# Gated linear attention and a rational feed-forward block on one core: a new order of the first loads, and 80 unread products ahead of the first sum

## The chip, the core and the metric

The kernel runs on one core of a Trainium2 chip. The engines of the core are TensorE (PE in the profile, its weight loads PEld), VectorE (DVE), ScalarE (ACT), GpSimd (POOL) and SyncE (SP). SyncE, ScalarE and GpSimd also issue DMA transfers, each into a queue of its own. The metric is device time in microseconds (us), the median of several executions of one program.

## What is computed

For each of 4 batches and 8 heads of width 48, a state of 48 by 48 numbers runs over 768 steps: it is multiplied by a gate and gets the outer product of k and v added, and q reads it. The result, 3072 rows of 384, goes through two matrix products with a rational function between them.

```python
f = 1.0 / (1.0 + np.exp(-f_logit))
for t in range(S):
    state = f[:, :, t, :, None] * state + np.einsum('bhd,bhe->bhde', k[:, :, t], v[:, :, t])
    y[:, :, t] = np.einsum('bhd,bhde->bhe', q[:, :, t], state)
...
h = x @ w_in                                   # 3072x384 by 384x2048
P = a[0] + a[1] * h + a[2] * h2 + a[3] * h3
Q = 1.0 + np.abs(b[0]) * np.abs(h) + np.abs(b[1]) * h2
return (P / (Q + 1e-06)) @ w_out               # 3072x2048 by 2048x384
```

## The kernel before

The work is cut into 12 units of 256 steps of one batch (3 stretches of time by 4 batches). A unit is done in chunks, so that the recurrence becomes matrix products. Its steps, by the names that the order uses:

- `ld n f|k|q|v` loads an input of unit n. An input lies in the memory as 8 heads; the numbers behind it (`0 2`, `2 4`) pick half of the heads. f, k and q are issued by SyncE; v is issued by GpSimd and is turned into bf16 on its way.
- `ef`, `ls` (ScalarE, L289 and L294): exponential and logarithm of the gate. `cs` (TensorE, L304, L308, L312): the running sums of these logarithms by products with triangular matrices `Ui` and `Us`; L312 is a group of products with only 4 columns. `A` (ScalarE, L326): exponentials of the sums.
- `xa n x` (VectorE or GpSimd, L331): k (x = 1) or q (x = 0) times `A`, into the tile `qkp`. `T` transposes it on TensorE (L345), `Te` copies it back, `sc` forms scores (L368), `mk` masks them (VectorE, L376). `ic` and `si` form the new state (TensorE, L434 and L444), `st` scales it (VectorE, L459). `yb` and `yi` form the output rows (L389), `ye` writes them out as `x`.
- `h` (TensorE, L469) is the product with `w_in`; 16 blocks of 128 columns, so `h 0 8 12` is blocks 8 to 11 of unit 0. Steps on VectorE, ScalarE and accumulating DMAs make the rational function, `o` (L549) is the product with `w_out`, `so` the store.
- `wi a 8 16` loads one of four row groups of the second half of `w_in` (L215, GpSimd); the first product `h 0 8 12` needs all four. `ab_ b` and `ab_ a` load the coefficients (L226), `fa` works on b.
- `cu 0`, `cu 1` and `ci` build `Ui`, `Us` and the identity on GpSimd; `cz` and `cm` fill zeros and the mask on VectorE.

The order of all steps is written out by hand in one table, `ORDER`. Each engine runs its own instructions in the order of the table, and waits by semaphores. `!m0` behind a step sets a mark, `^m0` behind another makes its DMA wait until the marked step is done. `@3` is the PSUM slot (of four) that a step takes. The first five rows of the table of before are these; the whole first unit, and the beginning of the second, lie in them:

```python
cu 1; cz 1; ld 0 f 2 4; ld 0 v; ab_ b s; cz 3; cz 0; ld 0 f 0 2; ci; ld 0 q 2 4; ld 1 f; cu 0; ld 0 k 0 2
ef 0 2 4; ls 0 2 4; cm; ld 0 k 2 4; cz 2; fa; cs 0 2 4 @0; ef 0 0 2; ls 0 0 2; ld 0 q 0 2; cs 0 0 2 @1; ld 1 k
A 0 1 0 2; A 0 1 2 4; A 0 0 2 4; A 0 0 0 2; fr; ld 2 f; ef 1; xa 0 1 2 4; ls 1; xa 0 0 2 4; vm 0 v; cs 1 @2
xa 0 0 0 2; ld 1 q; xa 0 1 0 2 !m0; ld 1 v ^m0; ld 3 f; ic 0 @3; wi 2 8 16; A 1 1; wi 3 8 16; A 1 0
T 0 0 2 @0; st 0 0; ld 2 q; ab_ a s; wi 1 8 16; xa 1 1 2 4; T 0 2 4 @1; wi 0 8 16; Te 0 0 2 s; sc 0 0 @2
```

So the load of v of unit 1 waits until the last product `xa 0 1 0 2` of unit 0, and the four loads of `w_in` stand behind it in GpSimd's queue.

Of the kernel before, what the change touches and what calls it, by code (L numbers as in the profile page):

```python
# [8 lines left out]
F32 = mybir.dt.float32  # L9
# [7 lines left out]


ORDER = """
cu 1; cz 1; ld 0 f 2 4; ld 0 v; ab_ b s; cz 3; cz 0; ld 0 f 0 2; ci; ld 0 q 2 4; ld 1 f; cu 0; ld 0 k 0 2  # L20
ef 0 2 4; ls 0 2 4; cm; ld 0 k 2 4; cz 2; fa; cs 0 2 4 @0; ef 0 0 2; ls 0 0 2; ld 0 q 0 2; cs 0 0 2 @1; ld 1 k
A 0 1 0 2; A 0 1 2 4; A 0 0 2 4; A 0 0 0 2; fr; ld 2 f; ef 1; xa 0 1 2 4; ls 1; xa 0 0 2 4; vm 0 v; cs 1 @2
xa 0 0 0 2; ld 1 q; xa 0 1 0 2 !m0; ld 1 v ^m0; ld 3 f; ic 0 @3; wi 2 8 16; A 1 1; wi 3 8 16; A 1 0
T 0 0 2 @0; st 0 0; ld 2 q; ab_ a s; wi 1 8 16; xa 1 1 2 4; T 0 2 4 @1; wi 0 8 16; Te 0 0 2 s; sc 0 0 @2
xa 1 0 0 2; Te 0 2 4 s; xa 1 0 2 4; ef 2; si 0 1; sc 0 1 @0; xa 1 1 0 2; st 0 1; T 1 @1; mk 0 0; ld 2 k
mk 0 1; yb 0 0 2 @3; yi 0 1; Te 1; ef 3; yb 0 2 4; ic 1 @2; ls 2; st 1 0 !m1; sc 1 1 @0; ld 2 v ^m1; ye 0 s
cs 2 @1; mk 1 1 !m4; ls 3; sc 1 0 @3; wi 0 0 8; A 2 0; si 1 1; ld 5 f; cs 3 @0; wi 3 0 8; st 1 1; A 2 1
# [75 lines left out]
def _at(t, dims, off=0):  # L103

    return bass.AP(tensor=t.tensor, offset=t.offset + off, ap=[t.ap[0]] + [list(d) for d in dims])
# [3 lines left out]
def kernel(  # L109
# [12 lines left out]
    nc = tc.nc  # L122
    B, H, S, D = q.shape
    C = 128
    P = 128
# [23 lines left out]
    Us = consts.tile([P, P], BF16, name="Us")  # L149
# [37 lines left out]
    def unit(n):  # L187
        if n not in units:
            c, b = divmod(n, B)
            units[n] = dict(n=n, c=c, b=b, qk=qkp[n % 2], ls=lsp[n % 2], vm=vmp[n % 2])  # L190
        return units[n]
# [5 lines left out]
    def slot(i, shape, dtype, name):  # L197
        return slots[i].tile(shape, dtype, name=name, tag="s")
# [46 lines left out]
    def const_z(i):  # L245
        if i < 2:
            nc.vector.memset(lsp[i][:, :, :, D:E], 0.0)
            nc.vector.memset(qkp[i].rearrange("p x i h d -> p (x i h) d")[:, :, D:E], 0.0)
            nc.vector.memset(vmp[i][:, :, :, 16:32], 0.0)
        elif i == 2:  # L250
            nc.vector.memset(ind, 0.0)
            for j in range(UB):
                nc.vector.memset(ind[R * j:R * j + R, j, :], 1.0)
        else:
            nc.vector.memset(hsel, 0.0)
            for r in range(2):
                nc.vector.memset(hsel[E * r:E * r + E, :, :, 1 - r], 1.0e4)
# [199 lines left out]
    def st(n, j):  # L457
# [3 lines left out]
            s["sv"][:, j].rearrange("p (b w) (r d) -> p b (w r) d", b=2, r=2),  # L461
            _at(s["ae"], [[DM + 16 if n else DM // 2 + 8, 2], [1, 4], [0, D]], 4 * j))

    def h(n, m0, m1, sl):
        s = unit(n)
        t = s["hp", m0] = slot(sl, [P, 4, NT], F32, "hp")
        for m in range(m0, m1):
            for kk in range(KD):
                nc.tensor.matmul(t[:, m - m0, :].rearrange("f (j t) -> f j t", j=UB),  # L469
                                 w_in_sb[:, kk, m * P:(m + 1) * P], s["x"][:, :, kk, :],  # L470
                                 start=(kk == 0), stop=(kk == KD - 1))
# [98 lines left out]
    def behind(i, mark):  # L570
# [2 lines left out]
                          reason="begins behind it")  # L573

    steps = dict(ld=load, wi=load_w_in, wo=load_w_out, ab_=load_ab, cu=const_u, ci=const_i, cm=const_m,
                 cz=const_z, fa=coef_a, fb=coef_b, fr=coef_r, tab=tab, ef=ef, ls=ls, cs=cs, A=A, xa=xa, T=T, Te=Te,
                 sc=sc, mk=mk, vm=vm, yi=yi, yb=yb, ic=ic, si=si, ye=ye, st=st, h=h, hy=hy, sq=sq, sa=sa, ab=ab,
                 zv=zv, zd=zd, rq=rq, p1=p1, p2=p2, pm=pm, ta=ta, tv=tv, gm=gm, o=o, oe=oe, so=store)
    for step in ORDER.replace("\n", ";").split(";"):
# [41 lines left out]
```

## Time and profile before

| | |
|---|---|
| median of 3 runs | 210.68 us (208.77 to 211.42) |
| profiled execution | 210.19 us |
| its span, from the first to the last instruction | 208.5 us |
| instructions on TensorE | 2894 products, 2894 weight loads |
| DMA traffic | 43.15 MB, 207 GB/s on the mean |

The profile is of one execution. A row of its timeline gives the start, the busy time, the engine, the source line and the operation, then how many instructions were merged into the row; in square brackets stands how long the engine was idle ahead of it and what ended that wait. "issue" means that nothing which the profile records ended it. Times in such rows count from the start of the span; the profiled execution's own time is 1.69 us more than its span.

### The profile page before, as it was taken

The page shows a single profiled execution, that of the slowest core. Times are in us where ns is not written, and L with a number is a line of the kernel's source. Part 1 is how long each engine was busy: PE and PEld are TensorE (multiplying, and loading weights), DVE is VectorE, ACT ScalarE, POOL GpSimd, SP SyncE. Part 2 cuts the span into 40 slices and gives each one's busy share as a digit, 9 for nine tenths or more (in the row PEclk, how much of TensorE's full clock was granted, in tenths as well). Part 3 has the DMA queues.
Part 4 walks back from the last instruction along what each step waited for, and adds up shares of the span by engine and source line. Part 5 has one row for each costly group of instructions (what it writes and reads, how often), then busy time and mean ns, then how long its engine had stood idle before and what let it go on. Part 6 is the DMA issues. An engine that isn't in the chain of part 4 may idle for free.

```text
span 208.5 us, 6605 instructions
## 1 busy us (share of the span) xinstructions
PE 191.0 (92%) x2894; PEld 139.4 (67%) x2894; DVE 187.0 (90%) x235; ACT 186.1 (89%) x172; POOL 77.8 (37%) x99
## 2 busy tenths in 40 slices
PE   1297799989999999999999999999999999999991
PEld 1165487867767778766888677678766766776650
DVE  3378579999999999999999989999999999999970
ACT  4756389999999999999999999999999999999871
POOL 6060610516961535026151760641674433412000
PEclk9999699999999999999999999999999999999998
DMA  6999999799999499999999999899999999998955
GB/s 98 287 300 186 271 220 253 186 220 233 168 206 202 85 176 152 249 267 265 208 222 252 250 199 229 209 200 210 185 191 163 214 211 195 193 190 183 238 146 167
DMA packets 61820, 43.15 MB, mean 207 GB/s; under 512 B 51424, under 2 KB 56544, under 8 KB 61792
## 3 DMA queue, kind: packets, MB, share of 16 engines
q0 software_dynamic: 20528, 23.86, 69.3%
q1 hardware_dynamic: 41184, 18.78, 34.7%
q8 instruction: 22, 0.36, 0.6%
q10 hardware_dynamic: 80, 0.10, 0.2%
q14 instruction: 6, 0.05, 0.1%
HBM read 25.17 MB, written 4.72 MB: 143 GB/s over the span
## 4 chain that ended last, share of the span: by engine, by line
PE 75%; DVE 10%; DMA 6%; SPq 4%; issue 2%; ACT 1%; DVEq 0%
PE op L549 31%; PE hp L469 26%; PE y L389 6%; SPq L209 4%; PE cs L304 3%; DMA v<-in_v_dram 3%; PE tp L345 3%; PE sc L368 2%; DMA q<-in_q_dram 2%; DVE scm L376 2%; DVE g L528 2%; PE sv L434 2%; DVE state L459 1%; PE sv L444 1%; DVE qkp L331 1%
## 5 line engine op out<-in xcount | busy, mean ns | idle before, releaser
L549 PE MATMUL op<-w_out_sb,g 128*128 128x384 bf16 x384 | 68.6, 326 | 0.0
L469 PE MATMUL hp<-x,w_in_sb 128*128 128x256 bf16 x576 | 68.0, 273 | 0.3 <-DVE state L459 0.3
L469 PEld LDWEIGHTS <-w_in_sb 128*128 128x128 bf16 x576 | 55.4, 98 | 9.4 <-issue 0.7
L549 PEld LDWEIGHTS <-g 128*128 128x128 bf16 x384 | 35.8, 98 | 22.6 <-DVE g L540 0.4
L481 ACT CAST hy<-hp 128x1024 bf16<-128x1024 f32 x48 | 47.8, 1027 | 2.6 <-PE hp L469 2.3
L508 ACT ACTIVATE z<-z 128x4096 bf16<-128x4096 bf16 (+1 forms) x16 | 44.5, 2780 | 1.1 <-DVE z L499 1.1
L540 DVE TENSOR_TENSOR g<-g,z 128x2048 bf16<-128x2048 bf16 (+2 forms) x24 | 28.9, 1218 | 1.1 <-issue 0.6
L503 POOL DMA_DIRECT2D z<-h x20 | 20.6, 1077 | 24.7 <-ACT h L490 17.0
L528 DVE TENSOR_TENSOR g<-g,h 128x2048 bf16<-128x2048 bf16 (+1 forms) x21 | 28.8, 1373 | 0.1
L376 DVE TENSOR_TENSOR scm<-sc,mask 128x1024 bf16<-128x1024 f32 x24 | 28.8, 1216 | 0.0
L490 ACT ACTIVATE h<-hy 128x2048 bf16<-128x2048 bf16 (+1 forms) x13 | 26.8, 2073 | 0.0
L326 ACT ACTIVATE A<-cs 128x768 f32<-128x768 f32 (+3 forms) x26 | 19.0, 779 | 6.5 <-PE cs L312 6.5
L532 POOL DMA_DIRECT2D g<-hy x15 | 13.8, 943 | 28.3 <-DVE g L528 9.3
L304 PE MATMUL cs<-lsp,Ui 128*128 128x384 bf16 (+1 forms) x39 | 12.0, 371 | 10.1 <-ACT lsp L294 8.7
L518 DVE TENSOR_SCALAR g<-hy,a_sb 128x2048 bf16<-128x2048 bf16 (+1 forms) x23 | 18.9, 829 | 1.4 <-ACT hy L481 1.4
L331 POOL TENSOR_TENSOR qkp<-k,A 128x384 bf16<-128x384 f32 x11 | 11.0, 1025 | 23.6 <-DVE g L540 10.4
L523 DVE TENSOR_SCALAR hy<-hy,a_sb 128x2048 bf16<-128x2048 bf16 (+1 forms) x20 | 18.3, 915 | 0.4
L209 POOL DMA_DIRECT2D v<-in_v_dram x12 | 12.1, 1012 | 15.7 <-DVE qkp L331 8.3
L494 DVE TENSOR_SCALAR z<-hy 128x2048 uint16<-128x2048 uint16 (+1 forms) x21 | 15.8, 764 | 0.0
L459 DVE TENSOR_TENSOR state<-sv,A 128x384 bf16<-128x384 f32 x20 | 11.0, 552 | 4.5 <-PE sv L444 2.4
L389 PE MATMUL y<-scm,v 64*32 64x128 bf16 x384 | 14.0, 218 | 0.8 <-DVE scm L376 0.7
L331 POOL TENSOR_TENSOR qkp<-q,A 128x384 bf16<-128x384 f32 x10 | 10.0, 1010 | 11.5 <-ACT A L326 5.5
(70 smaller groups left out, 246.4 us busy)
## 6 DMA issues: line engine op xcount, KB each, us to landing
z<-h POOLq DMA_DIRECT2D x20, 512.0 KB, 7.5
g<-hy POOLq DMA_DIRECT2D x15, 512.0 KB, 7.8
f<-in_f_logit_dram SPq DMA_DIRECT2D x11, 384.0 KB, 5.8
k<-in_k_dram SPq DMA_DIRECT2D x11, 384.0 KB, 7.7
q<-in_q_dram SPq DMA_DIRECT2D x11, 384.0 KB, 7.8
v<-in_v_dram POOLq DMA_DIRECT2D x12, 192.0 KB, 7.7
out_dram<-f SPq DMA_DIRECT2D x12, 192.0 KB, 3.9
out_dram<-osb SPq DMA_DIRECT2D x10, 192.0 KB, 6.4
```

Of the source, the lines that this page charges most:

```text
L209: return eng.dma_start(out=s[what][:, hh].rearrange("p h i d -> p h (i d)"), in_=src[s["b"], hh, t0:t0 + NT, :].rearrange("h (p i) d -> p ...
L331: i = (nc.gpsimd if eng == "p" else nc.vector).tensor_mul(s["qk"][:, x, :, hh, 0:D], s["qk"[x]][:, hh].rearrange("p h i d -> p i h d"), s[ ...
L376: return nc.vector.tensor_mul(t, s["sc", g].rearrange("s r a i t -> s (r a) (i t)"), mb)
L389: nc.tensor.matmul(s["y"][32 * a:32 * a + 32, j, kk * C:kk * C + C].rearrange("e (i t) -> e i t", i=2), lhsT, rhs, start=(j, a) not in s[" ...
L469: nc.tensor.matmul(t[:, m - m0, :].rearrange("f (j t) -> f j t", j=UB), w_in_sb[:, kk, m * P:(m + 1) * P], s["x"][:, :, kk, :], start=(kk ...
L481: nc.scalar.copy(fl(big(s, "hy"), m0, m1), fl(s["hp", m0], 0, m1 - m0))
L490: return nc.scalar.activation(fl(big(s, "h2"), m0, m1), fl(big(s, "hy"), m0, m1), AF.Square)
L503: return nc.gpsimd.dma_start(out=fl(big(s, "z"), m0, m1), in_=fl(big(s, "h2"), m0, m1), accum_op=ALU.add)
L508: return nc.scalar.add_instruction(mybir.InstActivation(name=nc.get_next_instruction_name(), func=AF.Reciprocal, ins=[nc.scalar.lower_ap(f ...
L528: return nc.vector.tensor_mul(fl(big(s, "g"), m0, m1), fl(big(s, "g"), m0, m1), fl(big(s, "h2"), m0, m1))
L540: return nc.vector.tensor_mul(fl(big(s, "g"), m0, m1), fl(big(s, "g"), m0, m1), fl(big(s, "z"), m0, m1))
L549: nc.tensor.matmul(s["op", g][:, j, 0:DM], big(s, "g")[:, m, C * j:C * j + C], w_out_sb[:, m, :], start=(s["on", j] == 1), stop=(s["on", j ...
```

## The change

Three things, all in the first five rows of `ORDER`, and one new step:

- The loads of unit 0 stand in another order: both halves of f, then k and q of the second half, f of unit 1, then q and k of the first half. b is loaded by ScalarE and no longer by SyncE. v of unit 0 is issued behind the building of `Ui` and of the identity, and `Ui` is built ahead of the identity.
- The mark `m0`, behind which v of unit 1 is loaded, moves from the step `xa 0 1 0 2` to `st 0 0`.
- A step `dn 80 @3` stands ahead of `cs 0 2 4`: 80 products of `Us` with 4 of its own columns into PSUM slot 3. Nothing reads them.

```diff
-cu 1; cz 1; ld 0 f 2 4; ld 0 v; ab_ b s; cz 3; cz 0; ld 0 f 0 2; ci; ld 0 q 2 4; ld 1 f; cu 0; ld 0 k 0 2
+cu 1; cz 1; ld 0 f 2 4; ab_ b a; cu 0; cz 3; cz 0; ld 0 f 0 2; ci; ld 0 v; ld 0 k 2 4; ld 0 q 2 4; ld 1 f
...
-T 0 0 2 @0; st 0 0; ld 2 q; ab_ a s; wi 1 8 16; ...
+T 0 0 2 @0; st 0 0 !m0; ld 1 v ^m0; wi 2 8 16; wi 3 8 16; ld 2 q; ab_ a s; wi 1 8 16; ...
...
+    def dn(n, sl):
+        t = slot(sl, [P, 2, 512], F32, "dn")
+        for i in range(n):
+            nc.tensor.matmul(t[:, i % 2, 0:4], Us, Us[:, 0:4], start=True, stop=True)
...
-                 cz=const_z, fa=coef_a, fb=coef_b, fr=coef_r, tab=tab, ef=ef, ls=ls, cs=cs, A=A, xa=xa, T=T, Te=Te,
+                 cz=const_z, fa=coef_a, fb=coef_b, fr=coef_r, tab=tab, ef=ef, ls=ls, cs=cs, dn=dn, A=A, xa=xa, T=T, Te=Te,
```

On SyncE, at the start of the program, the rows move as follows. f_117, k_120 and q_123 are the tiles of unit 0, f_118 and k_121 those of unit 1; a row with `4x96` is half of the heads.

```order
-L209 DMA f_117<-in_f_logit_dram 128x4x96
-L226 DMA b_sb<-in_moe_b_dram 128x2
-L209 DMA f_117<-in_f_logit_dram 128x4x96
+L622 UNCONDITIONAL_BRANCH
+L209 DMA f_117<-in_f_logit_dram 128x4x96 x2
+L209 DMA k_120<-in_k_dram 128x4x96
 L209 DMA q_123<-in_q_dram 128x4x96
 L209 DMA f_118<-in_f_logit_dram 128x8x96
-L209 DMA k_120<-in_k_dram 128x4x96 x2
 L209 DMA q_123<-in_q_dram 128x4x96
+L209 DMA k_120<-in_k_dram 128x4x96
```

The load of b is gone from this queue, the second half of f stands directly behind the first, and the first half of k has moved behind the first half of q.

On GpSimd, at the start, v_126 is v of unit 0, v_127 that of unit 1.

```order
-L209 DMA v_126<-in_v_dram 128x8x96
-masks.py:197 MEMSET ident 128x128
-masks.py:199 AFFINE_SELECT ident<-ident 128x128
 masks.py:65 MEMSET Ui 128x128
 masks.py:66 AFFINE_SELECT Ui<-Ui 128x128
 L232 AFFINE_SELECT Ui<-Ui 128x128
+masks.py:197 MEMSET ident 128x128
+masks.py:199 AFFINE_SELECT ident<-ident 128x128
+L209 DMA v_126<-in_v_dram 128x8x96
 L209 DMA v_127<-in_v_dram 128x8x96
 L215 DMA w_in_sb<-in_moe_w_in_dram 32x3x1024 x4
```

Only the load of v_126 and the building of the identity have moved; v_127 and the four loads of `w_in` behind it stand where they stood, and what has changed for them is the step that v_127 waits for.

On TensorE the 160 new rows stand ahead of everything else; the last of them, with what follows, read:

```order
L468 LDWEIGHTS Us
L468 MATMUL dn<-Us 128x4
L304 LDWEIGHTS Ui
L304 MATMUL cs<-lsp_81,Ui 128x192
```

Behind them the order of TensorE is that of before, each row 160 places further on in its program.

More of the change, by code (lines that the diff above doesn't have):

```diff
@@ L19 @@
 ORDER = """
-cu 1; cz 1; ld 0 f 2 4; ld 0 v; ab_ b s; cz 3; cz 0; ld 0 f 0 2; ci; ld 0 q 2 4; ld 1 f; cu 0; ld 0 k 0 2
-ef 0 2 4; ls 0 2 4; cm; ld 0 k 2 4; cz 2; fa; cs 0 2 4 @0; ef 0 0 2; ls 0 0 2; ld 0 q 0 2; cs 0 0 2 @1; ld 1 k
+cu 1; cz 1; ld 0 f 2 4; ab_ b a; cu 0; cz 3; cz 0; ld 0 f 0 2; ci; ld 0 v; ld 0 k 2 4; ld 0 q 2 4; ld 1 f
+ef 0 2 4; ls 0 2 4; cm; ld 0 q 0 2; cz 2; fa; dn 80 @3; cs 0 2 4 @0; ef 0 0 2; ls 0 0 2; ld 0 k 0 2; cs 0 0 2 @1; ld 1 k
 A 0 1 0 2; A 0 1 2 4; A 0 0 2 4; A 0 0 0 2; fr; ld 2 f; ef 1; xa 0 1 2 4; ls 1; xa 0 0 2 4; vm 0 v; cs 1 @2
-xa 0 0 0 2; ld 1 q; xa 0 1 0 2 !m0; ld 1 v ^m0; ld 3 f; ic 0 @3; wi 2 8 16; A 1 1; wi 3 8 16; A 1 0
-T 0 0 2 @0; st 0 0; ld 2 q; ab_ a s; wi 1 8 16; xa 1 1 2 4; T 0 2 4 @1; wi 0 8 16; Te 0 0 2 s; sc 0 0 @2
+xa 0 0 0 2; ld 1 q; xa 0 1 0 2; ld 3 f; ic 0 @3; A 1 1; A 1 0
+T 0 0 2 @0; st 0 0 !m0; ld 1 v ^m0; wi 2 8 16; wi 3 8 16; ld 2 q; ab_ a s; wi 1 8 16; xa 1 1 2 4; T 0 2 4 @1; wi 0 8 16; Te 0 0 2 s; sc 0 0 @2
 xa 1 0 0 2; Te 0 2 4 s; xa 1 0 2 4; ef 2; si 0 1; sc 0 1 @0; xa 1 1 0 2; st 0 1; T 1 @1; mk 0 0; ld 2 k
```

## The prediction

> **What bounds the kernel now.** I read the page's shares and slices first, then a table of stretches, then the timeline of the first 27 us.
>
> ```profile
> PE 191.0 (92%) x2894; PEld 139.4 (67%) x2894; DVE 187.0 (90%) x235; ACT 186.1 (89%) x172; POOL 77.8 (37%) x99
> PE   1297799989999999999999999999999999999991
> PEclk9999699999999999999999999999999999999998
> 0.00:5.00 5.00, 0.45 (x4) 0.53 (x5) 1.86 (x15) 2.33 (x3) 3.25 (x13) 1.00 0.58 96
> 20.00:26.00 6.00, 4.64 (x77) 2.99 (x77) 3.03 (x5) 2.52 (x4) 3.10 (x5) 0.72 1.19 261
> 26.00:31.00 5.00, 5.00 (x124) 4.32 (x121) 3.53 (x8) 3.91 (x5) 1.03 (x2) 1.00 1.30 220
> 71.00:81.00 10.00, 10.00 (x173) 7.76 (x171) 9.96 (x11) 9.97 (x8) 5.50 (x7) 1.00 0.79 143
> ```
>
> A row of stretches gives the length, the busy time of TensorE, its weight loads, VectorE, ScalarE and GpSimd, then the granted clock, the DMA share and GB/s. From 26 us on TensorE has no gap to speak of (5.00 of 5.00, 10.00 of 10.00). So what the change is worth is how much earlier TensorE reaches the first product with `w_in`, which starts at 26.00; the 180 us behind it only shift. The DMA queues are full there (share over 1): loads that finish late are late because of what is ahead of them.
>
> ```profile
> 1.32 0.49 SPq L226 DMA_DIRECT2D b_sb<-in_moe_b_dram  x1
> 1.69 1.06 POOL L209 DMA_DIRECT2D v<-in_v_dram  x1
> 1.85 0.43 SPq L209 DMA_DIRECT2D f<-in_f_logit_dram  x1
> 3.97 0.52 ACT L294 ACTIVATE lsp<-f 128x384 bf16<-128x384 f32 x1
> 4.55 0.32 PE L304 MATMUL cs<-lsp,Ui 128*128 128x192 bf16 x1 [4.55 <-ACT lsp L294]
> 5.18 0.52 ACT L289 ACTIVATE f<-f 128x384 f32<-128x384 f32 x1 [0.69 <-DMA f<-in_f_logit_dram]
> 7.28 1.67 ACT L326 ACTIVATE A<-cs 128x384 f32<-128x384 f32 x4 [1.02 <-PE cs L312]
> 9.70 0.84 ACT L294 ACTIVATE lsp<-f 128x768 bf16<-128x768 f32 x1
> 10.05 0.56 DVE L331 TENSOR_TENSOR qkp<-k,A 128x384 bf16<-128x384 f32 x1 [3.42 <-DMA k<-in_k_dram]
> 10.60 0.48 PE L304 MATMUL cs<-lsp,Ui 128*128 128x384 bf16 x1 [3.35 <-ACT lsp L294]
> 11.60 0.55 DVE L331 TENSOR_TENSOR qkp<-k,A 128x384 bf16<-128x384 f32 x1
> 11.93 0.35 PE L312 MATMUL cs<-ind,lsp 128*128 128x4 bf16 x8
> 12.21 0.82 PE L434 MATMUL sv<-v,qkp 64*128 64x96 bf16 x16
> 12.46 0.92 POOL L209 DMA_DIRECT2D v<-in_v_dram  x1 [8.25 <-DVE qkp L331]
> 13.08 0.56 DVE L459 TENSOR_TENSOR state<-sv,A 128x384 bf16<-128x384 f32 x1 [0.93 <-PE sv L434]
> 13.37 2.22 POOL L215 DMA_DIRECT2D w_in_sb<-in_moe_w_in_dram x4
> 14.49 1.03 DVE L331 TENSOR_TENSOR qkp<-q,A 128x384 bf16<-128x384 f32 x2 [0.39 <-DMA q<-in_q_dram]
> 16.37 2.35 DVE L376 TENSOR_TENSOR scm<-sc,mask 128x1024 bf16<-128x1024 f32 x2
> 19.97 0.52 PE L434 MATMUL sv<-v,qkp 64*128 64x96 bf16 x16 [0.57 <-DMA v<-in_v_dram]
> 20.41 0.42 PE L368 MATMUL sc<-T 48*64 48x128 bf16 x16
> 22.19 0.32 PE L304 MATMUL cs<-lsp,Ui 128*128 128x384 bf16 x1 [1.36 <-issue]
> 26.00 2.78 PE L469 MATMUL hp<-x,w_in_sb 128*128 128x256 bf16 x24
> ```
>
> Four waits make the 26 us: the second half of f (ScalarE idle 0.69 us until 5.18), k of unit 0 (VectorE idle 3.42 us until 10.05), v of unit 1 (TensorE until 19.97), and 1.36 us until 22.19 that no recorded event ends.
>
> **The change part by part.**
>
> *b and the order of f.* SyncE issues the second half of f 0.53 us earlier (1.32 for 1.85), with neither b nor v ahead of it. ScalarE is busy with the first half until 4.49 (3.97 + 0.52), so the second can gain from 0 to 0.69 us; I take 0.6, near the upper end, since the issue alone gives 0.53. The first `A` starts at 6.7 for 7.28, and `ls 1`, which ended at 10.54, ends at 9.9 if f of unit 1 is there by 8.2: its issue has not moved, and less stands ahead of it. b's own issue lies on ScalarE in the wait ahead of 3.4 us and costs nothing; without that cover it would cost the 0.49 us of its row. v of unit 0, issued some 1.6 us later behind `Ui` and the identity, was wanted behind the products of 10.05, so it has room.
>
> *k and q of unit 0.* k of the second half moves from behind three loads to third place, and the 3.42 us wait goes; the last product on k then ends before 11.6 instead of at 12.15. What is late next is TensorE: `ic 0` cannot start before `cs 1` has ended, and `cs 1` starts behind `ls 1`. So of the 3.42 us only the 0.6 of ScalarE stay: `ic 0`, which ended at 13.03 (12.21 + 0.82), ends at 12.4, and `st 0 0` at 13.0 (13.64 before).
>
> *The mark.* The load of v of unit 1 was requested at 12.46, 0.31 us behind the end of `xa 0 1 0 2` at 12.15. Now it is behind `st 0 0`: 13.0 + 0.3 = 13.3, 0.85 us later. Queued behind the waiting request on GpSimd are the four loads of `w_in`; they shift by the same.
>
> ```profile
> v<-in_v_dram POOLq DMA_DIRECT2D x1, 192.0 KB, 7.5
> w_in_sb<-in_moe_w_in_dram POOLq DMA_DIRECT2D x2, 192.0 KB, 9.0
> DMA to landing us min/median/max: 7.5/8.2/9.4
> DMA to landing us min/median/max: 5.8/7.7/10.0
> ```
>
> These are the time to landing of that v, the mean of the last two of the four requests, and the bounds for all 8 loads of `w_in` and all 12 of v. With 7.5 us v would land at 20.8; SyncE's loads, which share the engines, are about half a us further on by then, so I take 7.2 and 20.5 (bounds 19.1 to 23.3). TensorE then does `ic 1` and `sc 1 1` in 0.86 us (19.97 to 20.83): 21.4. The other path to there, q of unit 1, then VectorE's masks (14.49 to 18.72), moves earlier with SyncE's queue and is not late.
>
> *The 80 products.* The nearest rows are those of L312, with the same weights' shape and 4 columns: 8 in 0.35 us at 11.93.
>
> ```profile
> L312 PE MATMUL cs<-ind,lsp x96: 164/164/167, 5.2 to 132.7; 128*128 128x4 bf16 x96
> L312 PEld LDWEIGHTS <-lsp 128*128 128x128 bf16 x16 | 0.7, 104 | 0.0
> 1.45 0.30 POOL L232 TENSOR_SCALAR_AFFINE_SELECT Us<-Us 128x128 bf16<-128x128 bf16 x1
> ```
>
> One product takes 0.164 us, so seven steps take 0.35 - 0.164 = 0.19 us: 0.027 us each. `Us` is there at 1.75; 80 x 0.027 + 0.16 = 2.3 us, to 4.1, ahead of the 4.49 at which the first sum could start. They hide behind the wait for f, and cost nothing. The upper bound is 0.104 us, a whole weight load each (a rival). [...]
>
> *What they may give: the clock.* 16 transposes took 1.89 us at the start and 1.07 later, so TensorE was at about half speed there, and at 0.72 on the mean again from 20 to 26.
>
> ```profile
> 12.96 1.89 PE L345 MATMUL tp<-ident,qkp 128*128 128x128 bf16 x16
> 16.11 1.07 PE L345 MATMUL tp<-ident,qkp 128*128 128x128 bf16 x16
> q8 instruction: 22, 0.36, 0.6%
> ```
>
> The 80 products end at 4.1 and the sums of unit 0 by about 6.6; then TensorE waits for `ls 1` as before (3.35 us), and I count on no gain at `cs 1`. [...]
>
> *The 1.36 us wait.* It stands at row 448 of TensorE's program. The page counts 22 packets of 0.36 MB for instructions, 16 KB each; 5788 rows in 0.36 MB make about 64 bytes, so a packet is 256 rows. I read the wait as program code that came late while the queues were full. TensorE went from row 192, just ahead of the transposes of 16.11, to row 448 in under 5 us. Now 160 rows stand in front, and the same places of the program are the old rows 32 (in the sums of unit 0, before 7.28) and 288 (in the output sums, behind the first mask, so after 17.5): over 10 us apart. So I count the wait as gone: the gain is 0 to 1.36, and I take 1.36.
>
> *The sum.* `cs 2` starts at 21.4 for 22.19. From there to the product with `w_in` it took 3.8 us at a low clock; unchanged, it starts at 25.2. The last `w_in` request started at 15.03 (13.37 + 3 x 0.555); with 9.0 to 9.4 us it landed at 24.0 to 24.4, and lands 0.85 later, by 25.2. Both paths meet there: even at full clock the weights hold it. 26.0 - 25.2 = 0.8 us gained, all passed on since TensorE is full behind. I give 0.1 back for v of unit 2 and the first half of `w_in`, which follow `ic 1`, 0.5 us later than before. The profiled execution took 210.19 us (span 208.5): 210.19 - 0.7 = 209.5. The median of the runs is 210.68, so by it 210.0; I stay with the execution from which the rows are.
>
> **The rivals.**
>
> *The clock holds (15%).* If the products keep TensorE at full speed through `cs 1` and `ic 0` (10.60 to 13.03), 1.2 us go there: v is requested at 12.1 and `w_in` lands near 23.9. The product starts at about 24.0, 2.0 us earlier: 208.2. For it: the products fill the time before 4.5. Against it: the 3.35 us gap.
>
> *v and `w_in` come too late (20%).* The mark now holds five loads back, and v is waited for already. If v takes the 10.0 us of the slowest row, it lands at 23.3, `cs 2` starts at 24.2 and the product at 28.0: 2.0 us later, 212.2. It decides from a landing at 21.3 (26.0 - 3.8 - 0.86), 8.0 us behind its request; the median row has 7.7. This is the case on the other side.
>
> *A whole weight load per product (8%).* 80 x 0.104 = 8.3 us, to 10.1; the first sums end near 11.1 to 11.8 and `A` starts some 4 us late. v is requested at 16.6 to 17.8, and `w_in`, with its 7.5 to 9.0 us, lands at 26.7 to 29.5: 1 to 3.5 us slower, 212.5 in the middle.
>
> *The unexplained wait stays (12%).* If it belongs to that place and not to the row's number, `cs 2` starts at 22.7: 0.5 us worse, 210.8, and the change has done nothing for the end.
>
> **How the numbers follow.** The forecast, 209.5 (208.6 to 210.4 by its bounds), has 45%. The range runs from the clock case with some execution-to-execution scatter, 207.4, to the late loads, 212.2; outside lie about a tenth on either side. A difference of 2% (4.2 us) is about what a measurement of this kernel can tell from no change. Faster than that needs the clock case and as much again: 8%. Slower needs the far end of the weight loads or of v, both at once or worse than any row: 7%. The rest, 85%, is within.
>
> **What would show it.** The 80 products end by 4.2 and the first sum starts at 4.5. The second `ef` starts at 4.5 to 4.7; the wait of VectorE for k is gone. v of unit 1 is requested near 13.3 and lands at 20.5. No wait ended by "issue" over 1 us stands ahead of `cs 2`. The first product with `w_in` starts at 25.2, and waits for a DMA if TensorE is there sooner. I am wrong if the products run past 5 us, if v lands after 21.3, or if TensorE has new gaps behind 26 us that eat what was won.

## The result, and the profile after

| | before | after |
|---|---|---|
| median of 20 runs each, us | 210.68 (208.07 to 214.41) | 213.81 (211.33 to 218.28) |
| ratio, after to before | | 1.0134, 95% interval 1.0093 to 1.0174 |
| profiled execution, us | 210.19 | 215.39 |
| its span, us, and mean granted clock of TensorE | 208.5, 0.988 | 213.7, 0.987 |

The changed kernel is slower by 1.3%, outside the predicted range (207.4 to 212.2) on its far side. The ratio leaves out executions more than 1.5% above the fastest of their kernel; the medians are over all.

(Source lines behind the new step stand six higher than before: the first product with `w_in`, L469, is L475, the last one, L549, is L555.)

The page of the kernel after has these lines: the busy shares, the granted clock in 40 slices, and the queue of the program's code.

```profile
PE 195.5 (92%) x2974; PEld 142.7 (67%) x2974; DVE 187.6 (88%) x235; ACT 186.3 (87%) x172; POOL 77.6 (36%) x99
PEclk9999799999999999999999999999999999999998
q8 instruction: 23, 0.38, 0.7%
```

The clock has one low slice, as before (7 tenths, 6 before), and its mean is the same to 0.001, so it doesn't hold the 5.2 us between these two executions. One code packet more is fetched (23 for 22). 0.7% of 16 engines' span is 23.9 us, or about 1.0 us of one DMA engine for each packet.

The table of stretches of the kernel after, with the columns as before: length, busy times of TensorE, weight loads, VectorE, ScalarE, GpSimd, then clock, DMA share and GB/s.

```profile
20.00:26.00 6.00, 3.92 (x99) 2.81 (x96) 2.91 (x3) 2.26 (x3) 1.65 (x3) 0.83 1.14 234
46.00:51.00 5.00, 3.34 (x68) 2.62 (x66) 3.06 (x5) 4.01 (x5) 1.00 (x1) 1.00 1.37 218
61.00:71.00 10.00, 8.57 (x163) 6.75 (x152) 8.95 (x13) 8.79 (x9) 4.25 (x5) 1.00 1.33 200
71.00:81.00 10.00, 10.00 (x109) 6.90 (x107) 10.00 (x12) 10.00 (x10) 3.67 (x4) 1.00 0.63 115
```

The same stretches of the kernel before, and two that the prediction did not show:

```profile
41.00:46.00 5.00, 4.37 (x118) 3.32 (x112) 4.99 (x6) 4.90 (x7) 1.07 (x2) 1.00 1.42 237
46.00:51.00 5.00, 4.72 (x68) 3.94 (x65) 4.53 (x6) 4.51 (x5) 2.32 (x4) 1.00 1.20 236
56.00:61.00 5.00, 4.54 (x128) 3.44 (x126) 4.92 (x7) 4.98 (x3) 3.69 (x5) 1.00 1.25 214
61.00:71.00 10.00, 10.00 (x136) 7.07 (x134) 10.00 (x13) 9.67 (x13) 2.87 (x3) 1.00 1.19 180
```

TensorE has holes far behind 26 us: 1.66 us of 5 at 46, 1.43 us of 10 at 61; in both the DMA share is over 1.3. From 71 on, where the row shown has 0.63, it is as good as full. Between 26 and 71 us the holes come to 4.4 us. In the kernel before they came to 1.8 us already: it was not full from 26 on, as the prediction read from two stretches, but from 61 on.

The timeline of the kernel after, cut to the rows that answer to the predicted steps:

```profile
0.84 0.43 ACTq L226 DMA_DIRECT2D b_sb<-in_moe_b_dram  x1
1.80 2.29 PE L468 MATMUL dn<-Us 128*128 128x4 bf16 x80 [1.80 <-POOL Us L232]
4.41 0.52 ACT L289 ACTIVATE f<-f 128x384 f32<-128x384 f32 x1 [2.32 <-DMA f<-in_f_logit_dram]
5.39 0.51 ACT L289 ACTIVATE f<-f 128x384 f32<-128x384 f32 x1
5.54 0.32 PE L304 MATMUL cs<-lsp,Ui 128*128 128x192 bf16 x1 [1.44 <-ACT lsp L294]
7.48 1.67 ACT L326 ACTIVATE A<-cs 128x384 f32<-128x384 f32 x4 [1.03 <-PE cs L312]
10.79 0.48 PE L304 MATMUL cs<-lsp,Ui 128*128 128x384 bf16 x1 [3.35 <-ACT lsp L294]
11.62 0.56 DVE L331 TENSOR_TENSOR qkp<-k,A 128x384 bf16<-128x384 f32 x1 [1.31 <-DMA k<-in_k_dram]
13.16 1.89 PE L345 MATMUL tp<-ident,qkp 128*128 128x128 bf16 x16
13.27 0.56 DVE L459 TENSOR_TENSOR state<-sv,A 128x384 bf16<-128x384 f32 x1 [1.09 <-PE sv L434]
14.14 0.91 POOL L209 DMA_DIRECT2D v<-in_v_dram  x1 [9.97 <-DVE state L459]
16.74 1.89 PE L345 MATMUL tp<-ident,qkp 128*128 128x128 bf16 x16
22.94 0.52 PE L434 MATMUL sv<-v,qkp 64*128 64x96 bf16 x16 [2.08 <-DMA v<-in_v_dram]
23.74 0.34 PE L304 MATMUL cs<-lsp,Ui 128*128 128x384 bf16 x1
27.77 2.78 PE L475 MATMUL hp<-x,w_in_sb 128*128 128x256 bf16 x24
49.56 0.52 PE L434 MATMUL sv<-v,qkp 64*128 64x96 bf16 x16 [1.66 <-DMA v<-in_v_dram]
63.12 0.51 PE L434 MATMUL sv<-v,qkp 64*128 64x96 bf16 x16 [0.90 <-issue]
203.26 1.29 DVE L546 TENSOR_TENSOR g<-g,z 128x1024 bf16<-128x1024 bf16 x2 [0.69 <-DMA g<-hy]
204.01 5.37 PE L555 MATMUL op<-w_out_sb,g 128*128 128x384 bf16 x32 [0.63 <-DVE g L546]
```

Read from the top: the products take 2.29 us and end at 4.09, but the first half of f comes a microsecond late (landed at 4.39 for 3.40), so the first sum starts at 5.54 (4.55 before). v of unit 1 is requested at 14.14 and waited for until 22.94. The 1.36 us wait ahead of `cs 2` is gone (23.74). The first product with `w_in` starts at 27.77 instead of 26.00. Then come three delays that the profile of before doesn't have at this size: v of unit 3 (1.66 us; 0.63 before), a wait at 63.12 that no recorded event ends, and the last accumulating DMA at 203.

Where the 5.2 us between the two profiled executions arise is seen from the start of the same instruction of TensorE in both. (A row number here counts TensorE's weight loads and products from the start of its program, without the added products.)

| TensorE reaches | before, us | after, later by | changed kernel, second profile (e4_after) | without products (e9) |
|---|---|---|---|---|
| first product with `w_in` (row 537) | 26.00 | 1.77 | 1.21 | -0.79 |
| state of unit 3 (row 1287) | 45.90 | 3.68 | 2.27 | -0.24 |
| row 1798 | 58.19 | 3.69 | 2.27 | -0.24 |
| row 1826 | 58.52 | 4.65 | 3.37 | -0.24 |
| row 5500 | 181.72 | 4.46 | 3.59 | -0.11 |
| output of the last unit (row 5730) | 199.10 | 5.24 | 4.14 | -0.12 |

### The profile page after: what moved, and what is told of

Read it like the earlier page. It is cut to its first block, busy times and chain, and to the rows that moved or that the text cites. A ratio compares the mean times of both kernels' runs of the same rounds, so it can differ in the third digit from the quotient of the medians.

```text
span 213.7 us, 6765 instructions
## 1 busy us (share of the span) xinstructions
PE 195.5 (92%) x2974; PEld 142.7 (67%) x2974; DVE 187.6 (88%) x235; ACT 186.3 (87%) x172; POOL 77.6 (36%) x99
## 4 chain that ended last, share of the span: by engine, by line
PE 55%; DVE 22%; DMA 13%; issue 6%; ACT 2%; POOL 0%; DVEq 0%; POOLq 0%; ACTq 0%
PE hp L475 19%; PE op L555 16%; DMA v<-in_v_dram 8%; PE cs L304 5%; PE y L389 4%; DVE g L546 4%; DVE g L534 4%; DMA g<-hy 4%; PE tp L345 3%; DVE g L524 2%; PE sv L434 2%; PE sc L368 2%; DVE scm L376 2%; DVE state L459 2%; DVE z L500 2%
## 5 line engine op out<-in xcount | busy, mean ns | idle before, releaser
L555 PE MATMUL op<-w_out_sb,g 128*128 128x384 bf16 x384 | 68.8, 326 | 0.6 <-DVE g L546 0.6
L475 PE MATMUL hp<-x,w_in_sb 128*128 128x256 bf16 x576 | 68.2, 273 | 1.1 <-ACT f L289 0.5
L475 PEld LDWEIGHTS <-w_in_sb 128*128 128x128 bf16 x576 | 55.3, 98 | 10.6 <-issue 1.7
L555 PEld LDWEIGHTS <-g 128*128 128x128 bf16 x384 | 35.8, 98 | 23.4 <-DVE g L546 1.2
L389 PE MATMUL y<-scm,v 64*32 64x128 bf16 x384 | 14.6, 225 | 0.0
L345 PE MATMUL tp<-ident,qkp 128*128 128x128 bf16 x192 | 14.4, 235 | 0.1
```

The lines of the kernel that those rows point to most:

```text
L345: nc.tensor.transpose(t[:, x, i, p, :], s["qk"][:, x, i, 2 * p:2 * p + 2, :].rearrange("t h d -> t (h d)"), ident)
L389: nc.tensor.matmul(s["y"][32 * a:32 * a + 32, j, kk * C:kk * C + C].rearrange("e (i t) -> e i t", i=2), lhsT, rhs, start=(j, a) not in s[" ...
L555: nc.tensor.matmul(s["op", g][:, j, 0:DM], big(s, "g")[:, m, C * j:C * j + C], w_out_sb[:, m, :], start=(s["on", j] == 1), stop=(s["on", j ...
```

## The experiments

Five theories were in play, and some expectations name them by a letter. M: the later mark makes v of unit 1 and `w_in` late. B: b's load runs beside f and delays it. C: the difference is TensorE's granted clock. F: the 160 new rows shift the places at which program code has to be fetched, and a fetch in a full queue makes TensorE or a load late. P: the products cost by their own work.

The four kernels of each group were timed beside runs of before of their own (medians 210.52, 211.43 and 210.56 us). The last column takes out the clock. Over the 235 executions of all kernels, one level for each kernel and one common slope, 1% of mean granted clock is worth 1.96 us (standard error 0.10; an execution scatters by 1.1 us around it). The column is a kernel's level less that of before, with two standard errors. (e12's median is high for its ratio: its mean clock was 0.984, for 0.990 in before.)

| run | what differs from before | median, us | ratio, 95% interval | at equal clock, us |
|---|---|---|---|---|
| e1_mark | mark | 211.65 | 1.0037 (0.9981 to 1.0093) | +0.6 ± 0.65 |
| e2_products | 80 products | 212.33 | 1.0102 (1.0048 to 1.0157) | +2.5 ± 0.9 |
| e3_loads | loads | 210.27 | 1.0010 (0.9972 to 1.0048) | -0.5 ± 0.7 |
| e4_after | all three | 213.74 | 1.0139 (1.0081 to 1.0197) | +1.9 ± 0.9 |
| e5_p128 | loads, 128 products | 210.90 | 1.0064 (1.0011 to 1.0117) | +0.15 ± 0.7 |
| e6_p80 | loads, 80 products | 210.77 | 1.0055 (1.0000 to 1.0111) | +1.2 ± 0.65 |
| e7_gap | 80 products in a later gap | 211.75 | 1.0101 (1.0034 to 1.0168) | +1.8 ± 0.9 |
| e8_b_behind_f | loads, b behind f | 209.70 | 0.9998 (0.9953 to 1.0042) | -0.5 ± 0.7 |
| e9_no_products | loads, mark | 210.66 | 1.0027 (0.9984 to 1.0071) | -0.45 ± 0.7 |
| e10_after_p128 | loads, mark, 128 products | 212.12 | 1.0120 (1.0066 to 1.0174) | +1.3 ± 0.7 |
| e11_p32 | loads, 32 products | 209.92 | 0.9999 (0.9961 to 1.0037) | +0.2 ± 0.7 |
| e12_b_behind_f_mark | loads, b behind f, mark | 214.26 | 1.0060 (1.0001 to 1.0119) | +1.2 ± 0.7 |

The changed kernel itself stands at +2.4 ± 0.55 in that column.

### The three parts, each alone

e1_mark is the kernel before with the new mark alone:

```diff
-xa 0 0 0 2; ld 1 q; xa 0 1 0 2 !m0; ld 1 v ^m0; ld 3 f; ic 0 @3; wi 2 8 16; A 1 1; wi 3 8 16; A 1 0
+xa 0 0 0 2; ld 1 q; xa 0 1 0 2; ld 3 f; ic 0 @3; A 1 1; A 1 0
-T 0 0 2 @0; st 0 0; ld 2 q; ...
+T 0 0 2 @0; st 0 0 !m0; ld 1 v ^m0; wi 2 8 16; wi 3 8 16; ld 2 q; ...
```

> Before, with the mark of the changed kernel alone: v of unit 1 and the four loads of w_in wait for the step st 0 0; loads and TensorE as before. Theory M (the mark): in the changed kernel v of unit 1 was requested at 14.14 for 12.46 and landed at 22.9 for 19.9, and the first product with w_in came 1.8 us later; so this kernel alone loses 1.5 to 3 us against before, ratio 1.007 to 1.014, and v lands behind 21.3. Theory B (b and f): the first half of f came 1 us late and everything hangs on that; then this kernel stays within 0.3% of before. Theory C (the clock): how long TensorE runs at the low clock decides, which this edit doesn't touch; within 0.3%.

e2_products is the kernel before with the products alone, ahead of the same sum:

```diff
-... cz 2; fa; cs 0 2 4 @0; ...
+... cz 2; fa; dn 80 @3; cs 0 2 4 @0; ...
```

> Before, with the 80 products alone. Theory M: they end before the first sum, and cost nothing; the wait of 1.36 us marked issue ahead of cs 2 is gone; ratio 0.993 to 1.000. Theory C: the products move the phase of TensorE's work against the clock, and the low clock lasts longer at the start; ratio 1.005 to 1.015. Theory B: 1.000.

e3_loads is the kernel before with the new order of the loads alone, b on ScalarE:

```diff
-cu 1; cz 1; ld 0 f 2 4; ld 0 v; ab_ b s; cz 3; cz 0; ld 0 f 0 2; ci; ld 0 q 2 4; ld 1 f; cu 0; ld 0 k 0 2
+cu 1; cz 1; ld 0 f 2 4; ab_ b a; cu 0; cz 3; cz 0; ld 0 f 0 2; ci; ld 0 v; ld 0 k 2 4; ld 0 q 2 4; ld 1 f
-ef 0 2 4; ls 0 2 4; cm; ld 0 k 2 4; cz 2; ... ls 0 0 2; ld 0 q 0 2; ...
+ef 0 2 4; ls 0 2 4; cm; ld 0 q 0 2; cz 2; ... ls 0 0 2; ld 0 k 0 2; ...
```

> Before, with the new order of the first loads alone (b by ScalarE, v behind the constants); the mark as before, no products. Theory B: the first half of f lands near 4.4 for 3.4, A starts no earlier than 7.3, and the kernel is slower than before by 0.5 to 1.5%. Theory M: the late f costs only what the earlier second half wins, A starts within 0.3 us of before, and the ratio is 0.996 to 1.003. Theory C: 1.000.

e4_after is the changed kernel once more, for a second profile:

> The changed kernel again, on the chip of the three others, for a profile that compares with theirs. All theories: ratio 1.009 to 1.018. M: v of unit 1 lands behind 21.3 again. C: the low clock at the start lasts past 18 us again; if it ends sooner and the time is the same, C falls.

The products alone cost 1.0%, the changed kernel 1.4%, the mark and the loads nothing that these intervals show. So the part that was counted at nothing carries most of the loss. (For the mark more can be said when its five pairs of kernels are taken together, below.) M had put e1_mark at 1.007 to 1.014 and B e3_loads at 1.005 to 1.015; both missed. C had named 1.005 to 1.015 for e2_products, by a longer low clock; the number came, but not by the clock: its mean was 0.992, for 0.991 in before beside it. The timeline of e2_products shows on TensorE and VectorE where it is lost:

```profile
1.80 2.29 PE L468 MATMUL dn<-Us 128*128 128x4 bf16 x80 [1.80 <-POOL Us L232]
4.57 0.32 PE L304 MATMUL cs<-lsp,Ui 128*128 128x192 bf16 x1 [0.47 <-ACT lsp L294]
26.21 2.57 PE L475 MATMUL hp<-x,w_in_sb 128*128 128x256 bf16 x22 [1.17 <-issue]
60.36 0.67 PE L434 MATMUL sv<-v,qkp 64*128 64x96 bf16 x16 [1.19 <-issue]
202.06 1.29 DVE L546 TENSOR_TENSOR g<-g,z 128x1024 bf16<-128x1024 bf16 x2 [0.93 <-DMA g<-hy]
```

The first sum starts at 4.57 as before (4.55), so the products' own work doesn't delay it. The 1.36 us wait has left `cs 2`, but 1.17 us of the same kind stand inside the first product with `w_in`, 1.19 us at 60.36, and the last accumulating DMA is late. The second profile of the changed kernel shows the same late places, and v of unit 1 late as well:

```profile
22.58 0.52 PE L434 MATMUL sv<-v,qkp 64*128 64x96 bf16 x16 [2.98 <-DMA v<-in_v_dram]
61.84 0.52 PE L434 MATMUL sv<-v,qkp 64*128 64x96 bf16 x16 [1.02 <-issue]
202.16 1.29 DVE L546 TENSOR_TENSOR g<-g,z 128x1024 bf16<-128x1024 bf16 x2 [0.47 <-DMA g<-hy]
```

### The number of products, their place, and b

e5_p128 and e6_p80 both have the new loads and the old mark, and differ in the number of products; in the row of `ORDER` only this changes:

```diff
-... dn 80 @3; cs 0 2 4 @0; ...
+... dn 128 @3; cs 0 2 4 @0; ...
```

> The changed kernel with the mark where it was before, and 128 products in place of 80, so that 256 rows and not 160 stand ahead of TensorE's program, one whole packet of its code. Theory F (the fetch of program code): the waits and the fetches behind them hang on which steps of the program lie at rows 192 + n x 256; with 256 rows more these are the steps of before again. So the wait of about 1 us at 60 us (row 1984 with 80 products) goes, the one ahead of cs 2 comes back, and the ratio to before is 1.000 to 1.006, though there are more products. Theory P (the products themselves, or what they do to the clock): 128 cost at least what 80 do, ratio 1.010 to 1.018.

> The changed kernel with the mark where it was before: the new loads and 80 products. Theory F and theory P: 1.008 to 1.013, the loads (1.001) and the products (1.010) together; F adds that TensorE waits about 1 us at row 1984, near 60 us, and that a fetch of code near 9 us leaves one of the 16 landings of a load of k about 1 us behind. If the mark is what costs (theory M), the ratio is that of the loads alone, 0.998 to 1.004.

e7_gap is the kernel before with the 80 products behind the sums of unit 0, in the 3.35 us in which TensorE waits for `ls 1`:

```diff
-... ls 0 0 2; ld 0 q 0 2; cs 0 0 2 @1; ld 1 k
+... ls 0 0 2; ld 0 q 0 2; cs 0 0 2 @1; dn 80 @3; ld 1 k
```

> Before, with the 80 products not ahead of the first sum but behind the sums of unit 0, in TensorE's wait of 3.35 us there. Theory F: the later program is shifted by the same 160 rows, so the wait at row 1984 comes and the ratio is 1.006 to 1.013. Theory C (the clock): TensorE now goes into cs 1 without a gap, the clock is high from about 11 instead of 16 us, and the ratio is below 0.998.

e8_b_behind_f has the new loads, no products, the old mark, and b in SyncE's queue behind both halves of f:

```diff
-... ld 0 f 2 4; ab_ b a; cu 0; cz 3; cz 0; ld 0 f 0 2; ci; ...
+... ld 0 f 2 4; cu 0; cz 3; cz 0; ld 0 f 0 2; ab_ b s; ci; ...
```

> The new order of the first loads with the mark as before and no products, and with b in SyncE's queue behind the second half of f, not on ScalarE's beside the first. Theory B (b beside f holds the first half of f up): the first half lands at 3.4 again, the second near 4.2, the first A starts at 6.6 to 6.8 for 7.28, and the ratio is 0.992 to 0.999. If something else holds A back, A starts at 7.2 or later, and the ratio is 1.000 or more.

128 products cost no more than 80 here (ratios 1.0064 and 1.0055), where P wants more. These two intervals alone are too wide to exclude P. All 235 executions together say more: a fit with one term for each part of the change, beside the clock, gives 2.0 ± 0.4 us for 80 products, 1.1 ± 0.6 us less for 128, and -0.5 ± 0.4 us for the loads. It takes the parts to add up, which e9 and e12 do not quite bear out (0.8 us below and above it). So P is improbable, and 128 products are probably cheaper than 80, though not free.

The timeline of e7_gap shows that filling the gap does not help either:

```profile
7.16 2.27 PE L468 MATMUL dn<-Us 128*128 128x4 bf16 x80
10.68 0.48 PE L304 MATMUL cs<-lsp,Ui 128*128 128x384 bf16 x1 [1.25 <-ACT lsp L294]
13.14 1.89 PE L345 MATMUL tp<-ident,qkp 128*128 128x128 bf16 x16
61.41 0.51 PE L434 MATMUL sv<-v,qkp 64*128 64x96 bf16 x16 [1.19 <-issue]
201.76 1.29 DVE L546 TENSOR_TENSOR g<-g,z 128x1024 bf16<-128x1024 bf16 x2 [0.52 <-DMA g<-hy]
```

The wait shrinks from 3.35 to 1.25 us, yet `cs 1` still takes 0.48 us and the transposes at 13.14 1.89 us, as in before (1.07 for the transposes at 16.11 there). The granted clock of that slice of e7's page is 9 tenths or more. In this kernel the products stand in another place, and the losses at 61 and 202 are there all the same. What the two kernels share is that everything behind stands 160 rows further on.

The timeline of e8_b_behind_f, on ScalarE, TensorE and GpSimd:

```profile
3.47 0.52 ACT L289 ACTIVATE f<-f 128x384 f32<-128x384 f32 x1 [1.38 <-DMA f<-in_f_logit_dram]
6.54 1.67 ACT L326 ACTIVATE A<-cs 128x384 f32<-128x384 f32 x4 [1.02 <-PE cs L312]
10.17 0.48 PE L304 MATMUL cs<-lsp,Ui 128*128 128x384 bf16 x1 [3.67 <-ACT lsp L294]
11.00 0.91 POOL L209 DMA_DIRECT2D v<-in_v_dram  x1 [6.81 <-DVE qkp L331]
```

f lands in time again (3.45; 4.39 in after), `A` starts at 6.54 (7.48 with b on ScalarE) and `cs 1` at 10.17 for 10.60. The first `ef` starts at 4.41 to 4.47 in after, e4, e5, e9 and e10, which have b on ScalarE, and at 3.42 to 3.47 in before, e1, e2 and e8, which don't. So B is right about f. But the time doesn't follow: 0.9998 for 1.0010, within both intervals.

e6_p80's profile, of an execution with a clock of 0.974, shows another load late than v:

```profile
21.77 0.84 ACT L289 ACTIVATE f<-f 128x768 f32<-128x768 f32 x1 [5.31 <-DMA f<-in_f_logit_dram]
23.40 0.48 PE L304 MATMUL cs<-lsp,Ui 128*128 128x384 bf16 x1 [2.88 <-ACT lsp L294]
```

Here v of unit 1, requested at 11.04 behind the old mark, is there in time, and f of unit 2 sets `cs 2`. The wait at row 1984 that F expected is there, at 63.68, but takes 0.31 us, not 1.

### Loads and mark without products, and other numbers

e9_no_products is the changed kernel less its 80 products, e10_after_p128 the changed kernel with 128, e11_p32 is e6 with 32, and e12_b_behind_f_mark is e8 with the new mark:

```diff
 e9:  -... dn 80 @3; cs 0 2 4 @0; ...
      +... cs 0 2 4 @0; ...
 e10: +... dn 128 @3; cs 0 2 4 @0; ...
 e11: +... dn 32 @3; cs 0 2 4 @0; ...
 e12: +... ld 0 f 0 2; ab_ b s; ci; ...   and   st 0 0 !m0; ld 1 v ^m0; wi 2 8 16; wi 3 8 16; ...
```

> The changed kernel without the 80 products: the new loads and the new mark. Theory F (what the products cost is where the fetches of code fall): no wait at the row of the step that had it near 60 us, no late accumulation near 202 us; ratio 0.998 to 1.006, over half of the change's loss gone. If the mark is the main cost (theory M): 1.008 to 1.013.

> The changed kernel with 128 products in place of 80, everything else as it is. Theory F: 256 rows bring the packets of code back to the steps of before; ratio 1.002 to 1.009, nearer to the kernel without products than to the changed one, and no wait over 0.5 us marked issue near 60 us. Theory P (the products themselves): 1.013 to 1.02.

> The new loads, the mark as before, and only 32 products (64 rows). Theory F: the steps at rows 192 + n x 256 are now the old rows 384, 1664 and 1920, and between 1408 and 1664 TensorE takes 4.5 us where a fetch needs some 6; so it waits 1 us or more at row 448 (before the last output sums of unit 0, near 19 us) and at row 1728 (near 56 us), and the ratio is 1.003 to 1.012, no better than with 80 and worse than with 128. Theory P: 32 products cost 0.4 of what 80 do, 1.000 to 1.004, and no such waits.

> The loads with b behind the second half of f, no products, and the new mark: a try at a kernel that beats both. A starts near 6.8 as with the old mark, v of unit 1 is requested near 13.2 for 11.0. Theory M: the later request costs 0.3 to 0.6% against the same kernel with the old mark, ratio 1.002 to 1.006. If the request is still early enough, and the loads of f and q behind it land sooner instead: 0.992 to 0.999.

e9 answers the main question: without the products no difference from before is shown (1.0027, 0.9984 to 1.0071), with them the ratio is 1.0134 (1.0093 to 1.0174), and the two intervals don't meet. The timeline of TensorE in e9:

```profile
20.24 0.52 PE L434 MATMUL sv<-v,qkp 64*128 64x96 bf16 x16 [1.06 <-DMA v<-in_v_dram]
21.37 0.48 PE L304 MATMUL cs<-lsp,Ui 128*128 128x384 bf16 x1 [0.27 <-PE sc L368]
25.21 2.78 PE L475 MATMUL hp<-x,w_in_sb 128*128 128x256 bf16 x24
45.65 0.51 PE L434 MATMUL sv<-v,qkp 64*128 64x96 bf16 x16 [1.20 <-DMA v<-in_v_dram]
```

v of unit 1 lands at 20.19, `cs 2` starts at 21.37 and the product with `w_in` at 25.21: to 0.3 us what was predicted for the change. That is in part luck: the request came at 14.21, 0.9 us later than predicted, and the transfer took 6.0 us for 7.2. And the 1.36 us wait is down to 0.27 us although no row has moved: TensorE waits for v just ahead of it, and that covers it. Of the 0.79 us won there, v of unit 3 takes back 0.55 (1.20 us of wait for 0.63 before).

e10 missed what F expected. Its profile has nothing at 61 and 202, as F says for a shift by a whole 256 rows, and the wait ahead of `cs 2` is back at its old place:

```profile
20.05 0.52 PE L434 MATMUL sv<-v,qkp 64*128 64x96 bf16 x16 [0.22 <-DMA v<-in_v_dram]
22.82 0.50 PE L304 MATMUL cs<-lsp,Ui 128*128 128x384 bf16 x1 [1.90 <-issue]
```

But its ratio of 1.0120 is that of the changed kernel within the intervals, and F wanted less than 1.009, so what its 128 products cost beside e9 is not explained by those two places. e11 missed too: its waits at such rows stand at others (960, 1984 and 4032, 2.6 us together, in an execution with a clock of 0.995) than were named for it, and it costs nothing (0.9999). e12 is no gain: v of unit 1 landed at 23.96 there, without any products. No version was shown to be faster than before.

## Why the prediction was wrong

**What failed: products "hide behind the wait for f, and cost nothing", and "the 180 us behind it only shift".** In their own place the products do hide: 2.29 us, to 4.09, as worked out. But 80 of them cost 1.0 to 1.1% in e2, in e7, and in after against e9; only beside the new loads with the old mark it is less (0.45%, e6 against e3). And TensorE was not full behind 26 us, so that a delay, or a gain, was not simply passed on: in e9 v of unit 3 took back most of what was won. The prediction added up TensorE's time and never asked what 160 more rows in front do to a program that is fetched while it runs (in after 23 code packets, from 9.18 to 198.67 us). It had used just this fetch to explain the 1.36 us wait.

How the rows cost is shown in part. TensorE's waits marked "issue" stand, to a few rows, at rows 192 + 256 n of its program: row 448 in before, 704 and 1984 in e2, 960 and 1984 in after. The packets of the instruction queue show what ends them. The first packet goes with row 448, the next with row 704, and so on. In all fourteen profiles there are 13 such waits of 0.3 us or more, and every one stands at such a row and ends 2.3 to 2.6 us behind the start of that row's packet. The packet itself started 3.1 to 4.5 us after TensorE had passed the row 256 further up. None of the 302 passages of such a row came sooner than 2.17 us behind its packet. So these are waits for program code. They do not come with added rows alone: e1_mark, without any products, has two, at rows 1728 and 1984 of its own program:

```profile
62.00 0.25 PE L368 MATMUL sc<-T 48*64 48x128 bf16 x3 [0.66 <-issue]
68.74 2.02 PE L475 MATMUL hp<-x,w_in_sb 128*128 128x256 bf16 x17 [1.44 <-issue]
```

What added rows change is which steps stand at those places. The first five kernels of this table have 80 products, e9 has none, and e10 has 128, so that its rows are shifted by a whole 256.

| lost against before, us | after | e4 | e2 | e7 | e6 | e9 | e10 |
|---|---|---|---|---|---|---|---|
| from row 1798 to row 1826 | 0.96 | 1.10 | 1.26 | 1.26 | 0.37 | 0.00 | 0.00 |
| from row 5500 to row 5730 | 0.78 | 0.55 | 1.02 | 0.60 | 0.18 | -0.01 | -0.01 |

In the first line the new row 1984 stands between the two places. In the second, the trace has a code packet at 198.7 us (after), 199.9 (e4), 199.7 (e2), 199.5 (e7) and 201.6 (e6), when the last accumulating DMA is on its way, and the last of that DMA's sixteen parts lands 0.7 to 1.6 us behind the fifteenth. In the nine other kernels it lands at most 0.4 us behind. Eight of these fetch their last packet before that DMA is issued, and e11, with a packet at 199.1, when it has landed. These two places make 1.7 to 2.3 us in four of the five profiles with 80 products, against 1.8 to 2.5 us at equal clock for the same kernels; in e6, which loses least of them by its ratio, they make 0.6. That is no full balance: the 1.36 us wait of before is gone from its place, other waits ahead of 28 us came for it, and e10 is slow without either loss. e8 and e12, without products, also lose 0.8 us in the first line, but there the wait for v ends it, and not "issue".

289 of the 302 passages had no wait of 0.3 us or more; the 13 waits took 0.3 to 1.9 us each, and here such waits and late packets decided.

**The wait of 1.36 us, "counted as gone".** At its place it went in the kernels with 80 products, but in e9, with no row moved, it went too (0.27 us left), so the shift is not the only thing that removes it. What failed is that it counted as a gain of the whole: in e2 1.17 us stood inside the first product with `w_in`, and as much again at 60.

**The mark.** The request was put at 13.3 and the landing at 20.5; they were 14.14 and 22.90 (14.16 and 22.54 in e4). 0.8 us of the miss is the request: `A` started 0.8 us later than taken (below), and with it `ls 1`, `cs 1` (10.79) and `st 0 0`. The rest is the transfer, 8.8 and 8.4 us where 7.2 was taken. The rival "v and `w_in` come too late" had its break-even at 21.3 and the product at up to 28.0; it started at 27.77 and 27.21. So this rival was right about the first 28 us, and its 212.2 misses what follows them. Yet e9 has the same mark, the same request (14.21) and a landing at 20.19, while e12, with the mark and no products, has 23.96. The mark does not make v late every time; it takes away the room for a late one. Beside 80 products it costs some 1.7 us (1.0134 against e6's 1.0055), without them 0.35 us (e9 against e3); the intervals overlap in both pairs. But in all five pairs of kernels that differ in the mark alone (the others are e1 and before, e10 and e5, e12 and e8) the one with it is the slower, by 0.2 to 0.8%. The fit over all executions puts the mark at 0.8 ± 0.4 us, or 0.6 ± 0.45 with a level of its own for each group of runs. So it was not free either.

**f and b.** `A` was to start at 6.7 and started at 7.48, because b was costed by its issue alone. The issue is hidden on ScalarE as predicted, but 1 KB of b in the other queue delayed the landing of the first half of f from 3.40 to 4.39; with b behind f (e8) it is 3.45. Seen at the end this was worth nothing measurable.

**Right:** the products' own duration; no gain at `cs 1` (0.48 us before and after; the 3.35 us wait stayed and the transposes still took 1.89 us). That it is this wait which undoes a gain is not shown: in e7 it is 1.25 us, and both times are the same. Right, too: TensorE as late as before behind VectorE's wait for k. That wait itself did not go, as predicted, but fell from 3.42 to 1.31 us, and the last product on k ended at 12.18, not before 11.6. The 0.7 us that were to be gained are neither shown nor excluded for loads and mark without the products: e9 has a gain of 0.45 ± 0.7 us at equal clock, but a ratio of 1.0027.

**The granted clock** (C) explains much of the scatter between executions and little of the difference: the mean clock of before is 0.990 and that of after 0.987, 0.6 us by the slope, of 3.1 us between the medians.

**What stays open.** Why v of unit 1 takes 5.2 (e8) to 9.3 us (e12) from request to landing. The sixteen parts of that load land within 1.6 to 2.7 us of each other in before, e9, e10 and e1, and spread over 3.3 to 4.7 us in after, e4, e6 and e12, and over 3.8 us in e7. Several parts come late, not one: more than 1.5 us behind the first are six in after, eight in e6 and seven in e12, for two in before. A code packet some microseconds ahead does not decide it: after, e4, e6 and e2 have one at about 9 us, and in e2 the parts land within 1.3 us; e12 has the spread without one. Open, too, are how the 2 to 3 us split between the two late places and the late loads, and why e10 is as slow as it is. There is one profile of each kernel, two of the changed one.

## What to carry to other kernels

Instructions that do nothing and hide in a wait need not be free: in this long program, with a DMA share of 1.04 from 27.4 us on, they moved every later place at which code is fetched, and 80 of them cost 2.0 ± 0.4 us by the fit. Before adding such filler, look for waits marked "issue" in the profile, count the rows between them, and see which tight steps and loads the fetches will fall on after the shift. Before counting on a full engine, look at every stretch behind the change, not at two. And leave room in front of a load that is already waited for: a mark moved later by what the median transfer allows (7.7 us) leaves none for a slow one: v took 6.0 us in e9 and 8.8 in after.

## What the runs showed of the hardware

- A code packet of 16 KB took 0.88 to 1.66 us in before and after, 0.96 in the middle. It started 3.1 to 4.5 us after TensorE had passed the row 256 further up, at the 13 rows where TensorE then waited, and TensorE went on 2.3 to 2.6 us behind its start: 5.5 to 6.9 us in all. The waits were 0.3 to 1.9 us.
- When such a packet fell into an accumulating DMA of 512 KB, the last of its sixteen parts landed 0.7 to 1.6 us behind the fifteenth (five profiles; 1.03 us in after), for at most 0.4 us in the nine others (0.36 in before).
- 1% of mean granted clock was worth 1.96 us of some 210. The low stretch is 3.41 us at half clock in before (22.49 to 25.90) and in after (23.98 to 27.39), 0.8% of the span; by that slope one more or less makes some 1.6 us, an estimate.
- 80 products in 2.27 to 2.29 us of otherwise idle time made TensorE's next rows no shorter: behind those ahead of the first sum its first product took 0.32 us (after), as in before; behind those in the gap ahead of `cs 1` (e7) the first product of `cs 1` took 0.48 us, as in before, where one of the same shape took 0.34 us at 42.86. The transposes behind took 1.89 us in before, after and e7, for 1.07 at 16.11 in before. Nor did the 3.58 us of 128 products (e10): the first sum right behind them took 0.32 us, the transposes 1.89. The granted clock stands at 1.00 in these stretches of before (5 to 22.49 us) and after (5 to 23.98), so its record doesn't hold these longer times.
- The load of b, 1 KB on a second queue, delayed the half of f, 192 KB, that was issued beside it by 1.0 us: it landed at 4.39 us in after, at 3.40 in before and at 3.45 in e8.
